# A planned fp32 attention and MoE kernel: new costs in the plan, idle transposes as filler, and one addition moved from ACT to DVE

## The chip, the cores and the metric

The kernel runs on one core of a Trainium2 chip. The metric is device microseconds of an execution; lower is better. The engines are PE (TensorE, matmuls and transposes), DVE (VectorE), ACT (ScalarE), POOL (GpSimd) and SP (SyncE, which here issues the DMAs). Each engine works through its own queue in order and waits at an instruction for the semaphores of others.

## What is computed

```
scores = q @ k.T / sqrt(64), causal mask, softmax:  attn = exp(s - max) / (sum + 1e-9)
x = (attn @ v) of 2 x 12 heads, 448 positions, 64 wide   -> 896 tokens x 768
x = ((x @ w1) * (x @ w2)) @ w3 @ w_out                   (768 -> 1024 -> 1024 -> 768)
h = x @ v_in ;  out = (h * clip(h + 3, 0, 6) / 6) @ v_out  (768 -> 2048 -> 768)
```

All weights arrive as 64-bit floats and are turned on the chip into pairs of fp32 parts, high and low. A dense product is three matmuls on these parts.

## The kernel before, in words

Attention works on 12 units of two heads each. A unit has seven score tiles `s_6` to `s_0` (128 rows, 448 down to 64 columns). For each, PE makes the scores in one of three PSUM banks (L431), DVE takes the scaled and masked minimum (L434), and ACT takes the exponential and its sum (L438). For tiles 6 to 4 and then 3 to 0, ACT adds 1e-9 to the sums (L450), DVE takes the reciprocal (L452), and POOL scales the exponentials in place (L458, tile `prb`). PE then transposes 16 blocks in four groups `ptp_0` to `ptp_3` (L480), ACT and DVE copy them out (L488, L492), and PE multiplies by v (`o`, L505).

Beside it runs the product `w3 @ w_out` (`pw`, 384 matmuls, L568), whose weights are loaded (L255) and converted by ACT, DVE and POOL (L261 to L295: L292 shifts the low word, L295 joins the words, L261 and L267 split the result). What of `pw` doesn't fit beside attention follows it. Then come the dense parts: `pa` (x @ w1 and x @ w2, by Strassen's scheme, L703), `px` (L812), `pg` (L703) and `po` (L877).

The order of instructions on each engine is not written out by hand. A planner, `Plan`, records every operation with an engine, an assumed cost in us, what it reads and writes, and a rank. `issue` then plays it through: whichever engine is free first takes, of its operations whose inputs are ready, the one of lowest rank, and the instructions are emitted in that order. So a changed cost moves instructions on every engine. `LATENCY` is what a result takes to reach another engine. PSUM and SBUF buffers go round in rings; an operation that opens a buffer waits for the last reader of the one before in it. Before any of this, `setup` makes the identity and issues 20 transposes of it (L410, tile `warm`).

Of the kernel before, what the change touches and what calls it, by code (L numbers as in the profile page):

```python
# [9 lines left out]
F32 = mybir.dt.float32  # L10
# [12 lines left out]
DENSE_BANKS = 2  # L23
# [25 lines left out]

WARM = 20  # L50
SHAPE = (2, 12, 448, 64)
# [21 lines left out]
class Plan:  # L73
# [3 lines left out]

    LATENCY = {"pe": 0.2, "sp": 2.2}

    def __init__(self):  # L80
        self.ops = []
        self.tags = {}

    def tile(self, make, tag, bufs, after=()):
        return Handle(self, make, tag, bufs, after)

    def op(self, eng, cost, fn, reads=(), writes=(), rank=0.0, after=()):
        i = len(self.ops)
        deps = set(after)
        args = [(*(a if isinstance(a, tuple) else (a, None)), w)  # L90
# [15 lines left out]
    def issue(self):  # L106
        n = len(self.ops)
        deps = [set(o[3]) for o in self.ops]
        for bufs, hs in self.tags.values():
            for x, h in enumerate(hs):  # L110
                first = h.uses[0][0]
                if x >= 1:
                    deps[first].add(hs[x - 1].uses[0][0])
# [15 lines left out]
        here = {e: [] for e in engines}  # L129
        free = {e: 0.0 for e in engines}  # L130
        for i in range(n):
            if not left[i]:
                heapq.heappush(coming[self.ops[i][0]], (0.0, i))
        for _ in range(n):
            t, e = min(
                (free[e] if here[e] else max(free[e], coming[e][0][0]), e)
                for e in engines if here[e] or coming[e]
            )
# [5 lines left out]
            free[e] = t + self.ops[i][1]  # L144
            for j in after[i]:
                near = self.ops[j][0] == e and e != "sp"
                ready[j] = max(ready[j], free[e] + (0.0 if near else self.LATENCY.get(e, 0.12)))
                left[j] -= 1
                if not left[j]:
                    heapq.heappush(coming[self.ops[j][0]], (ready[j], j))  # L150
        return max(free.values())
# [3 lines left out]
def attention_moe_moe2(ctx: ExitStack, tc, q, k, v, w1, w2, w3, w_out, v_in, v_out, out):  # L155
# [102 lines left out]
    def split(plan, hl, at_, size, x, reads, rank, eng="dve"):  # L258
# [5 lines left out]
        else:  # L264
# [3 lines left out]
            hl[:, LO, at_:at_ + size], x(), f32(hl[:, HI, at_:at_ + size]), ALU.subtract),  # L268
            reads=[*reads, hl.at(("h", at_))], writes=[hl.at(("l", at_))], rank=rank)

# [6 lines left out]
    def bits(plan, raw, size, rank, shifted=False, packed=False):  # L277
# [12 lines left out]
        else:  # L290
            plan.op("dve", 0.16 + size * 0.00052,
                    lambda: nc.vector.tensor_single_scalar(lo(), lo(), 29, ALU.logical_shift_right),  # L292
                    writes=[lb], rank=rank)
        to = (lambda: flat(raw)[:, :size]) if packed else lo
        plan.op("dve", dve(size), lambda: nc.vector.scalar_tensor_tensor(  # L295
            to(), hi(), 3, lo(), ALU.logical_shift_left, ALU.bitwise_or),
            reads=[] if packed else [hb], writes=[lb, hb] if packed else [lb], rank=rank)

# [24 lines left out]
    def combine(plan, f, r1, r2, rank):  # L323
# [20 lines left out]
        def add(dst, reads, write, a, b, op):  # L344
            plan.op("dve", dve(h), lambda: nc.vector.tensor_tensor(dst(), a(), b(), op),
                    reads=reads, writes=[write], rank=rank)

# [38 lines left out]
    def load(u):  # L386
# [4 lines left out]
        vr[u] = tile_of("vr", 3, [P, 4, 2, D], f"vr{u}")  # L391
        plan.op("sp", 0.6, lambda: nc.sync.dma_start(qs[u][:, :], q[u]), writes=[qs[u]], rank=rank)
        plan.op("sp", 0.6, lambda: nc.sync.dma_start(ks[u][:, :], k[u]), writes=[ks[u]], rank=rank)
        plan.op("sp", 0.6, lambda: nc.sync.dma_start(vr[u][:, :], v[u]), writes=[vr[u]], rank=rank)

# [47 lines left out]
    def normalise(u, t0, t1):  # L443
# [51 lines left out]
    def p_v(u):  # L495
# [32 lines left out]
        xt[p, b] = t  # L528

    setup()  # L530
    for u in range(n_u):
# [424 lines left out]
```

## Time and profile before

| | |
|---|---|
| median of 3 runs | 553.81 us (553.14 to 557.26) |
| the profiled execution | 556.21 us, its span 554.4 us |
| PE busy | 540.8 us (98%), 2828 matmuls |
| DVE, ACT, POOL busy | 388.9, 301.6, 108.0 us |
| HBM | 75.24 MB read, 14.16 MB written |

Busy times are of the profiled execution. PE's matmuls overlap in the pipeline, so its busy time alone does not say that it works at its peak; the pace between starts, and the clock that it was granted, say more. The time in front of an instruction on which its engine did nothing is put down to whatever released it last.

### The profile page before, as it was taken

To read this page: it belongs to the slowest core of one execution; us is meant where nothing else is said; L and a number is where in the kernel's file an instruction comes from. 1 tells how busy PE (TensorE), PEld (TensorE's weight loads), DVE (VectorE), ACT (ScalarE), POOL (GpSimd) and SP (SyncE) were. 2 spreads that over 40 slices of the span, in tenths; PEclk is the share of its full clock that TensorE was granted. 3 is DMA by queue.
4 is the path that set the end of the run, shared out by engine and by line. 5 is a ranking of instruction groups with operands and counts; after the bars stand their busy time and mean duration, and the time that the engine had idled before them with its cause. 6 is when DMAs were issued, how large, how long until landed. Compare 5 with 4: busy or idle time off the path is not lost.

```text
span 554.4 us, 7965 instructions
## 1 busy us (share of the span) xinstructions
PE 540.8 (98%) x2828; PEld 480.3 (87%) x2828; DVE 388.9 (70%) x722; ACT 301.6 (54%) x606; POOL 108.0 (19%) x150
## 2 busy tenths in 40 slices
PE   7899999999999999999999999999999999999997
PEld 5576657778999999999999999999999999899996
DVE  3677777764962789888747549999978884876322
ACT  4587886785822555564526335996846651653000
POOL 4656456553101111111000102010101000000000
PEclk9899999999999999999999999999999999999999
DMA  8666785722713143422433011357384846572664
GB/s 314 245 201 228 226 278 206 232 92 72 228 44 96 61 151 145 156 99 97 170 96 115 0 58 67 124 209 240 110 314 139 276 164 194 175 252 80 204 188 143
DMA packets 33224, 89.91 MB, mean 162 GB/s; under 512 B 3232, under 2 KB 21664, under 8 KB 30624
## 3 DMA queue, kind: packets, MB, share of 16 engines
q1 hardware_dynamic: 33184, 89.40, 47.7%
q8 instruction: 22, 0.36, 0.3%
q14 instruction: 18, 0.15, 0.1%
HBM read 75.24 MB, written 14.16 MB: 161 GB/s over the span
## 4 chain that ended last, share of the span: by engine, by line
PE 75%; DVE 1%; issue 0%; ACT 0%; DVEq 0%
PE po L877 21%; PE paX L703 10%; PE px L812 10%; PE pgX L703 10%; PE pw L568 7%; PE paZ L703 5%; PE pgZ L703 5%; PE pgY L703 3%; PE paY L703 3%; PE o L505 0%; PE ptp L480 0%; DVE o L671 0%; DVE vja L267 0%; DVE q L841 0%; ACT q L838 0%
## 5 line engine op out<-in xcount | busy, mean ns | idle before, releaser
L877 PE MATMUL po<-g,vo 128*128 128x448 f32 x576 | 116.3, 362 | 0.0
L877 PEld LDWEIGHTS po<-g,vo 128*128 128x128 f32 x576 | 108.0, 187 | 7.2
L568 PE MATMUL pw<-wr,w 128*128 128x384 f32 x384 | 75.8, 347 | 0.0
L458 POOL TENSOR_SCALAR prb<-prb,sums 128x448 f32<-128x448 f32 (+6 forms) x84 | 59.5, 725 | 54.9 <-DVE sums L452 54.9
L568 PEld LDWEIGHTS pw<-wr,w 128*128 128x128 f32 x384 | 65.9, 188 | 1.7
L812 PE MATMUL px<-ab,wp 128*128 128x448 f32 x288 | 57.9, 362 | 0.0
L812 PEld LDWEIGHTS px<-ab,wp 128*128 128x128 f32 x288 | 54.0, 187 | 3.6
L431 PE MATMUL s<-ks,qs 128*128 128x448 f32 (+6 forms) x168 | 51.2, 415 | 4.3 <-DMA ks<-in_k 2.2
L671 DVE TENSOR_TENSOR o<-po,o 128x448 f32<-128x448 f32 x36 | 22.4, 623 | 40.7 <-PE po L877 38.9
L438 ACT ACTIVATE prb<-z,sums 128x448 f32<-128x448 f32 (+6 forms) x84 | 42.1, 506 | 5.6 <-DVE sums L434 5.5
L434 DVE CUSTOM_DVE_ANT_0 z<-s,maskb 128x448 f32<-128x448 f32 (+6 forms) x84 | 33.3, 418 | 15.7 <-PE s L431 11.4
L431 PEld LDWEIGHTS s<-ks,qs 128*128 128x128 f32 x168 | 28.4, 197 | 14.8 <-DVE sums L434 5.7
L261 POOL TENSOR_SCALAR vja<-vir 128x768 fp32r<-128x768 f32 x8 | 7.3, 914 | 169.6 <-DVE x2t L653 70.2
L488 ACT COPY pt<-ptp 128x512 f32<-128x512 f32 (+1 forms) x48 | 24.7, 562 | 15.8 <-PE ptp L480 15.6
L480 PEld LDWEIGHTS ptp<-ident,prb 128*128 128x128 f32 x192 | 22.4, 143 | 9.7 <-POOL prb L458 5.3
L480 PE MATMUL ptp<-ident,prb 128*128 128x128 f32 x192 | 26.4, 280 | 4.2 <-POOL prb L458 4.2
L505 PE MATMUL o<-pt,vr 128*64 128x448 f32 (+3 forms) x192 | 26.9, 396 | 0.0
L505 PEld LDWEIGHTS o<-pt,vr 128*64 128x64 f32 (+1 forms) x192 | 10.9, 134 | 17.5 <-issue 11.9
L265 ACT CAST vo<-vor 128x1024 fp32r<-128x1024 f32 x12 | 13.6, 1136 | 17.3 <-PE po L877 15.3
L285 ACT ACTIVATE vor<-vor 128x1024 f32<-128x1024 f32 x12 | 13.9, 1158 | 15.9 <-DMA vor<-in_moe_w_out 15.9
L664 DVE SCALAR_TENSOR_TENSOR g<-rab,g 128x448 fp32r<-128x448 f32 x32 | 20.6, 650 | 1.6 <-ACT g L662 1.6
L662 ACT ACTIVATE g<-rab 128x448 fp32r<-128x448 f32 x32 | 18.2, 576 | 5.4 <-DVE rab L660 5.4
(146 smaller groups left out, 1038.2 us busy)
## 6 DMA issues: line engine op xcount, KB each, us to landing
vor<-in_moe_w_out SPq DMA_DIRECT2D x12, 1024.0 KB, 5.6
w3r<-in_moe_w SPq DMA_DIRECT2D x8, 1024.0 KB, 6.6
sums_of<-o SPq DMA_DIRECT2D x36, 224.0 KB, 3.1
o<-sums_of SPq DMA_DIRECT2D x36, 224.0 KB, 2.8
wrr<-in_moe_w_out SPq DMA_DIRECT2D x8, 768.0 KB, 5.5
w1r<-in_moe_w SPq DMA_DIRECT2D x8, 768.0 KB, 5.6
w2r<-in_moe_w SPq DMA_DIRECT2D x8, 768.0 KB, 4.2
vjr<-in_moe_w_in SPq DMA_DIRECT2D x8, 768.0 KB, 5.0
```

What stands on the lines that cost most here:

```text
L431: plan.op("pe", pe4(n), lambda: nc.tensor.matmul(ps[:, :n], qs[u][:, t].rearrange("p h i -> p (h i)"), ks[u][:, :n], start=True, stop=True ...
L434: plan.op("dve", dve(n) + 0.09, lambda: nc.vector.tensor_tensor_reduce(out=z[:, :n], in0=ps[:, :n], in1=maskb[:, S - n:], scale=-SCALE, sc ...
L438: plan.op("act", act(n, True) + 0.2, lambda: nc.scalar.activation(pb[:, OFF[t]:OFF[t] + n], z[:, :n], AF.Exp, bias=sm[:, 0, t:t + 1], scal ...
L458: nc.gpsimd.tensor_scalar(s, s, sm[:, 1, t:t + 1], 1.0, ALU.mult, ALU.mult)
L480: nc.tensor.transpose(ps[:w, i * P:(i + 1) * P], pb[:, OFF[t] + kb * P:OFF[t] + kb * P + w], ident)
L488: plan.op("act", act(cut), lambda: nc.scalar.copy(dst()[:, :cut], ps[:, :cut]), reads=[ps], writes=[d.at((g, 0))], rank=rank)
L505: nc.tensor.matmul(ps[T * j:T * j + T, kb * P:S], vr[u][:w, kb, j, :], d[:w, base[kb]:base[kb] + TQ - 2 * kb, j, :], start=kb == 0, stop=k ...
L568: nc.tensor.matmul(ps[:, :W], weight(n, a, kk), hls[1 + kk][:, c, h * W:(h + 1) * W], start=kk == 0 and a == c, stop=kk == KF - 1 and a == LO)
L671: plan.op("dve", dve(S), lambda: nc.vector.tensor_tensor(o[:, :], ps[:, :S], o[:, :], ALU.add), reads=[ps], writes=[o], rank=rank)
L703: nc.tensor.matmul(ps[:, :S], hl[:, a, off + kk * P:off + (kk + 1) * P], t[:, c], start=first and kk == 0 and a == c, stop=kk == HK - 1 an ...
L812: nc.tensor.matmul(ps[m, b][:, :S], weight(n, a, kk), ab[kk][:, c, cols(b)], start=kk == 0 and a == c, stop=kk == KF - 1 and a == LO)
L877: nc.tensor.matmul(ps[:, :S], hls[n][:, a, at_:at_ + P], gt[k][:, d, cols(b)], start=kk == 0 and a == d, stop=kk == KC - 1 and a == LO)
```

## The change

Five things are changed.

1. The planner's costs. An engine can now start late (`START`: PE at 5.0 us, SP at 0.6). The loads of q, k and v cost 1.3, 0.7 and 0.8 us of SP instead of 0.6 each.
2. POOL's stands. DVE operations marked `ports=True` (those with two SBUF inputs, and the shift L292) lock POOL: one that POOL has begun ends later by their cost, and one that begins starts when they have ended. Two SP operations that are tied only by the order of a ring no longer have `LATENCY` between them.
3. The addition of 1e-9 goes from ACT (rank `early`) to DVE, ahead of the reciprocal.
4. `keep_warm` puts 60 transposes of the identity on PE with rank 1000, the last of all, into a bank of the ring that `pw` uses, and allows them from the first score on.
5. The transposes ahead of the first score become 18.

The core of the diff (the marks `ports=True` stand on L267, L292, L295, L345 and the differences of L597, too):

```diff
-WARM = 20
+WARM = 18
+
+FILL, IDLE = 60, 1000.0
...
     LATENCY = {"pe": 0.2, "sp": 2.2}
+    START = {"pe": 5.0, "sp": 0.6}
...
-        free = {e: 0.0 for e in engines}
+        free = {e: self.START.get(e, 0.0) for e in engines}
...
+        busy, locked = None, 0.0
+
+        def settle(i, end):
+            e = self.ops[i][0]
+            for j in after[i]:
+                near = self.ops[j][0] == e and (e != "sp" or (i, j) in order)
+                ready[j] = max(ready[j], end + (0.0 if near else self.LATENCY.get(e, 0.12)))
...
+            if busy and busy[1] <= t:
+                settle(*busy)
+                busy = None
+                continue
...
+            cost = self.ops[i][1]
+            if e == "pool":
+                free[e] = max(t, locked) + cost
+                busy = i, free[e]
+                continue
+            free[e] = t + cost
+            if i in self.ports:
+                locked = free[e]
+                if busy:
+                    free["pool"] = busy[1] + cost
+                    busy = busy[0], free["pool"]
+            settle(i, free[e])
...
-        plan.op("sp", 0.6, lambda: nc.sync.dma_start(qs[u][:, :], q[u]), writes=[qs[u]], rank=rank)
-        plan.op("sp", 0.6, lambda: nc.sync.dma_start(ks[u][:, :], k[u]), writes=[ks[u]], rank=rank)
-        plan.op("sp", 0.6, lambda: nc.sync.dma_start(vr[u][:, :], v[u]), writes=[vr[u]], rank=rank)
+        plan.op("sp", 1.3, lambda: nc.sync.dma_start(qs[u][:, :], q[u]), writes=[qs[u]], rank=rank)
+        plan.op("sp", 0.7, lambda: nc.sync.dma_start(ks[u][:, :], k[u]), writes=[ks[u]], rank=rank)
+        plan.op("sp", 0.8, lambda: nc.sync.dma_start(vr[u][:, :], v[u]), writes=[vr[u]], rank=rank)
...
-        early = u + (TQ - 1 - t0) * 0.05 + RANK["exp"]
         total = [sm.at((2, t)) for t in range(t0, t1)]
-        plan.op("act", 0.22, lambda: nc.scalar.activation(
-            sm[:, 2, t0:t1], sm[:, 1, t0:t1], AF.Copy, bias=1.0e-9, scale=1.0), reads=acc, writes=total, rank=early)
+        plan.op("dve", 0.17, lambda: nc.vector.tensor_single_scalar(sm[:, 2, t0:t1], sm[:, 1, t0:t1], 1.0e-9, ALU.add),
+                reads=acc, writes=total, rank=rank)
...
+    def keep_warm(after):
+        ps = plan.tile(lambda: pd.tile([P, 512], F32, tag="d", name="warm"), "psd", DENSE_BANKS)
+        for i in range(FILL):
+            plan.op("pe", 0.11, lambda: nc.tensor.transpose(ps[:, :P], ident, ident), writes=[ps], rank=IDLE, after=after)
...
     attended = len(plan.ops)
+    keep_warm([min(i for i in range(attended) if plan.ops[i][0] == "pe")])
```

What this does to the order is shown at three places. The first is the start of the kernel, on SP and DVE. `qs1`, `ks1` and `vr1` are q, k and v of unit 1, `w3r0` and `wrr0` the first raw weights. SP before:

```order
L392 DMA qs0_132<-in_q 128x896
L393 DMA ks0_134<-in_k 128x448
L394 DMA vr0_136<-in_v 128x512
L255 DMA w3r0_138<-in_moe_w3 128x2048
L392 DMA qs1_147<-in_q 128x896
L393 DMA ks1_156<-in_k 128x448
L394 DMA vr1_162<-in_v 128x512
```

SP after:

```order
L424 DMA qs0_130<-in_q 128x896
L425 DMA ks0_132<-in_k 128x448
L426 DMA vr0_134<-in_v 128x512
L424 DMA qs1_136<-in_q 128x896
L425 DMA ks1_138<-in_k 128x448
L426 DMA vr1_142<-in_v 128x512
L287 DMA w3r0_149<-in_moe_w3 128x2048
```

The three loads of unit 1 have moved ahead of `w3r0`. On DVE, `z0_2` is the minimum of score tile 2 of unit 0, and the row `sums0` behind it reads it out. DVE before, from the first `w3r0` operation on:

```order
L292 TENSOR_SCALAR w3r0_138<-w3r0_138 128x1024
L434 ISA z0_2_176,sums0_145<-s0_2_160,maskb_86 128x192
L434 ISA sums0_145 128x1
L434 ISA z0_1_179,sums0_145<-s0_1_167,maskb_86 128x128
L434 ISA sums0_145 128x1
L452 RECIPROCAL sums0_145<-sums0_145 128x3
L295 SCALAR_TENSOR_TENSOR w3r0_138<-w3r0_138 128x1024
```

DVE after, from the minimum of tile 4 of unit 1 on:

```order
L466 ISA z1_4_219,sums1_202<-s1_4_199,maskb_86 128x320
L466 ISA sums1_202 128x1
L481 TENSOR_SCALAR sums0_147<-sums0_147 128x4
L483 RECIPROCAL sums0_147<-sums0_147 128x4
L324 TENSOR_SCALAR w3r0_149<-w3r0_149 128x1024
L327 SCALAR_TENSOR_TENSOR w3r0_149<-w3r0_149 128x1024
L466 ISA z1_3_260,sums1_202<-s1_3_215,maskb_86 128x256
```

The two `w3r0` operations stand behind the second reciprocal of unit 0 now, and the new addition (L481) stands ahead of it.

The second place is PE from the middle of unit 1's scores to the first transposes of unit 0. Before:

```order
L431 MATMUL s1_3_213<-ks1_156,qs1_147 128x256
L431 MATMUL s1_2_219<-ks1_156,qs1_147 128x192
L431 MATMUL s1_1_223<-ks1_156,qs1_147 128x128
L431 MATMUL s1_0_236<-ks1_156,qs1_147 128x64
L480 MATMUL ptp0_0_238<-ident_85,prb0_87 128x128 x4
L480 MATMUL ptp0_1_247<-ident_85,prb0_87 128x128 x4
L431 MATMUL s2_6_257<-ks2_193,qs2_189 128x448
```

After:

```order
L463 MATMUL s1_3_215<-ks1_138,qs1_136 128x256
L564 MATMUL warm_160<-ident_85 128x128 x2
L463 MATMUL s1_2_222<-ks1_138,qs1_136 128x192
L564 MATMUL warm_160<-ident_85 128x128 x2
L463 MATMUL s1_1_229<-ks1_138,qs1_136 128x128
L564 MATMUL warm_160<-ident_85 128x128 x24
L463 MATMUL s1_0_271<-ks1_138,qs1_136 128x64
L564 MATMUL warm_160<-ident_85 128x128 x7
L463 MATMUL s2_6_288<-ks2_227,qs2_211 128x448
L511 MATMUL ptp0_0_298<-ident_85,prb0_87 128x128 x4
L511 MATMUL ptp0_1_307<-ident_85,prb0_87 128x128 x4
```

35 of the 60 idle transposes stand in these rows, 14 ahead of them and 11 behind, and the first score of unit 2 has moved ahead of the transposes.

The third place is PE in the middle of attention, at the first transposes of unit 3 (`ptp3`). Before:

```order
L431 MATMUL s4_3_546<-ks4_375,qs4_369 128x256
L568 MATMUL pw0_1_331<-wr3_513,w30_201 128x384 x3
L431 MATMUL s4_2_555<-ks4_375,qs4_369 128x192
L431 MATMUL s4_1_559<-ks4_375,qs4_369 128x128
L480 MATMUL ptp3_0_571<-ident_85,prb1_88 128x128 x4
L480 MATMUL ptp3_1_579<-ident_85,prb1_88 128x128 x4
L431 MATMUL s4_0_587<-ks4_375,qs4_369 128x64
L431 MATMUL s5_6_590<-ks5_468,qs5_457 128x448
```

After:

```order
L463 MATMUL s4_2_592<-ks4_417,qs4_397 128x192
L605 MATMUL pw0_0_449<-wr2_518,w30_294 128x384 x3
L463 MATMUL s4_1_603<-ks4_417,qs4_397 128x128
L605 MATMUL pw0_1_500<-wr2_518,w30_294 128x384 x3
L463 MATMUL s4_0_615<-ks4_417,qs4_397 128x64
L605 MATMUL pw0_0_449<-wr3_590,w30_294 128x384 x3
L463 MATMUL s5_6_631<-ks5_545,qs5_525 128x448
L511 MATMUL ptp3_0_643<-ident_85,prb1_88 128x128 x4
L511 MATMUL ptp3_1_651<-ident_85,prb1_88 128x128 x4
```

The transposes of unit 3 now stand behind `s4_0`, three more `pw` matmuls and `s5_6`. Of the `pw` matmuls 165 stood ahead of the last `o` before, and 156 do now.

## Rows read from the trace of the kernel before

**Rows 1.** The page: busy time of each engine.
```profile
PE 540.8 (98%) x2828; PEld 480.3 (87%) x2828; DVE 388.9 (70%) x722; ACT 301.6 (54%) x606; POOL 108.0 (19%) x150
```

**Rows 2.** Stretches: busy us and count of each engine; granted clock; DMA share and GB/s.
```profile
core 0: us, PE busy (x) PEld busy (x) DVE busy (x) ACT busy (x) POOL busy (x), PEclk, DMA share, GB/s
11.10:12.00 0.90, 0.89 (x2) 0.47 (x3) 0.71 (x3) 0.78 (x5) 0.90 (x1) 0.85 1.02 423
12.00:15.00 3.00, 3.00 (x7) 1.77 (x6) 1.35 (x5) 1.98 (x7) 2.27 (x4) 0.50 1.03 398
...
16.00:19.00 3.00, 0.43 (x2) 0.30 (x2) 3.00 (x13) 1.04 (x5) 3.00 (x5) 0.93 0.39 100
19.00:22.00 3.00, 2.92 (x10) 2.44 (x11) 0.45 (x1) 1.50 (x4) 2.83 (x5) 0.51 1.00 388
...
22.00:140.00 118.00, 114.39 (x699) 83.01 (x698) 82.99 (x236) 88.95 (x254) 63.07 (x87) 1.00 0.58 191
140.00:554.40 414.40, 410.64 (x2074) 385.40 (x2073) 295.50 (x450) 201.12 (x324) 31.96 (x33) 1.00 0.43 146
...
470.00:475.00 5.00, 4.84 (x23) 3.88 (x23) 4.67 (x6) 2.02 (x5) 1.36 (x1) 1.00 0.48 154
```

**Rows 3.** Timeline of PE, first 23 us: start, us, what, count, [idle before it <-releaser].
```profile
1.36 4.11 PE L410 MATMUL warm<-ident 128*128 128x128 f32 x20 [1.36 <-POOL ident masks.py:199]
5.31 3.60 PE L431 MATMUL s<-ks,qs 128*128 128x448 f32 x14
11.12 4.84 PE L431 MATMUL s<-ks,qs 128*128 128x448 f32 x12 [2.21 <-DMA ks<-in_k]
16.94 0.43 PE L431 MATMUL s<-ks,qs 128*128 128x64 f32 x2 [0.98 <-DVE sums L434]
19.08 1.97 PE L480 MATMUL ptp<-ident,prb 128*128 128x128 f32 x8 [1.70 <-POOL prb L458]
20.84 2.13 PE L431 MATMUL s<-ks,qs 128*128 128x448 f32 x4
```

**Rows 4.** Timeline of SP and DVE at the start; the two `ks` loads' time to landing.
```profile
1.17 0.42 SPq L393 DMA_DIRECT2D ks<-in_k  x1
3.06 0.45 SPq L393 DMA_DIRECT2D ks<-in_k  x1
...
DMA to landing us min/median/max: 3.4/5.6/7.9
...
9.25 0.70 DVE L292 TENSOR_SCALAR w3r<-w3r 128x1024 uint32<-128x1024 uint32 x1 [0.83 <-DMA w3r<-in_moe_w]
15.26 0.17 DVE L452 RECIPROCAL sums<-sums 128x4 f32<-128x4 f32 x1
```

**Rows 5.** Timeline of PE in the middle of attention.
```profile
37.50 1.04 PE L480 MATMUL ptp<-ident,prb 128*128 128x128 f32 x8
38.38 0.97 PE L431 MATMUL s<-ks,qs 128*128 128x448 f32 x2
...
47.80 1.09 PE L480 MATMUL ptp<-ident,prb 128*128 128x128 f32 x8 [1.11 <-POOL prb L458]
```

**Rows 6.** Waits of PE, whole span: us in total, times, longest us.
```profile
PE ptp L480 <- POOL prb L458: 4.2, 4, 1.7
PE s L431 <- DVE sums L434: 1.9, 3, 1.0
```

**Rows 7.** POOL's groups by form, 10 to 14 us (busy us, mean ns), and DVE's timeline.
```profile
L458 POOL TENSOR_SCALAR prb<-prb,sums 128x448 f32<-128x448 f32 x1 | 1.6, 1560 | 6.8 <-DVE sums L452 6.8
L458 POOL TENSOR_SCALAR prb<-prb,sums 128x384 f32<-128x384 f32 x1 | 0.6, 582 | 0.0
...
10.45 1.22 DVE L295 SCALAR_TENSOR_TENSOR w3r<-w3r 128x1024 uint32<-128x1024 uint32 x1
15.35 1.19 DVE L267 TENSOR_TENSOR w<-w3r,w 128x1024 fp32r<-128x1024 f32 x1
```

**Rows 8.** Lines L450 and L452: ns min/median/max; who waited for L452 (us, times).
```profile
L450 ACT ACTIVATE sums<-sums x24: 207/208/226, 9.0 to 126.8; 128x3 f32<-128x3 f32 x12, 128x4 f32<-128x4 f32 x12
L452 DVE RECIPROCAL sums<-sums x24: 156/170/179, 10.3 to 127.0; 128x3 f32<-128x3 f32 x12, 128x4 f32<-128x4 f32 x12
...
  POOL prb L458: 54.9, 21
```

**Rows 9.** Chain of waits in order of time: start us, us, what.
```profile
136.82 38.17 PE pw L568 x219
174.99 1.80 PE paX L703 x9
...
550.82 0.02 issue
```

More of the change, by code (lines that the diff above doesn't have):

```diff
@@ L82, in __init__, with op @@
         self.tags = {}
+        self.ports = set()
     def tile(self, make, tag, bufs, after=()):
         return Handle(self, make, tag, bufs, after)
-    def op(self, eng, cost, fn, reads=(), writes=(), rank=0.0, after=()):
+    def op(self, eng, cost, fn, reads=(), writes=(), rank=0.0, after=(), ports=False):
         i = len(self.ops)
+        if ports:
+            self.ports.add(i)
         deps = set(after)
@@ L108, in issue @@
         deps = [set(o[3]) for o in self.ops]
+        order = set()
         for bufs, hs in self.tags.values():
@@ L112, in issue @@
                 if x >= 1:
-                    deps[first].add(hs[x - 1].uses[0][0])
+                    before = hs[x - 1].uses[0][0]
+                    if before not in deps[first]:
+                        order.add((before, first))
+                    deps[first].add(before)
                 if x >= bufs:
@@ L133, in issue @@
                 heapq.heappush(coming[self.ops[i][0]], (0.0, i))
-        for _ in range(n):
-            t, e = min(
+        busy, locked = None, 0.0
[4 more added lines that the diff above has]
+                ready[j] = max(ready[j], end + (0.0 if near else self.LATENCY.get(e, 0.12)))
+                left[j] -= 1
+                if not left[j]:
+                    heapq.heappush(coming[self.ops[j][0]], (ready[j], j))
+        todo = n
+        while todo or busy:
+            t, e = min((
                 (free[e] if here[e] else max(free[e], coming[e][0][0]), e)
                 for e in engines if here[e] or coming[e]
-            )
+            ), default=(float("inf"), None))
+            if busy and busy[1] <= t:
+                settle(*busy)
+                busy = None
+                continue
             while coming[e] and coming[e][0][0] <= t:
@@ L143, in issue @@
             self.ops[i][2]()
[L144 to L150, printed above, removed]
+            todo -= 1
+            cost = self.ops[i][1]
[10 more added lines that the diff above has]
+            settle(i, free[e])
         return max(free.values())
@@ L268, in split @@
             hl[:, LO, at_:at_ + size], x(), f32(hl[:, HI, at_:at_ + size]), ALU.subtract),
-            reads=[*reads, hl.at(("h", at_))], writes=[hl.at(("l", at_))], rank=rank)
+            reads=[*reads, hl.at(("h", at_))], writes=[hl.at(("l", at_))], rank=rank, ports=True)
     def parts(name, m):
@@ L292, in bits @@
                     lambda: nc.vector.tensor_single_scalar(lo(), lo(), 29, ALU.logical_shift_right),
-                    writes=[lb], rank=rank)
+                    writes=[lb], rank=rank, ports=True)
         to = (lambda: flat(raw)[:, :size]) if packed else lo
@@ L296, in bits @@
             to(), hi(), 3, lo(), ALU.logical_shift_left, ALU.bitwise_or),
-            reads=[] if packed else [hb], writes=[lb, hb] if packed else [lb], rank=rank)
+            reads=[] if packed else [hb], writes=[lb, hb] if packed else [lb], rank=rank, ports=True)
     def convert(plan, n, rank):
@@ L345, in add @@
             plan.op("dve", dve(h), lambda: nc.vector.tensor_tensor(dst(), a(), b(), op),
-                    reads=reads, writes=[write], rank=rank)
+                    reads=reads, writes=[write], rank=rank, ports=True)
         L1, L2, H1, H2 = r1.at("l"), r2.at("l"), r1.at("h"), r2.at("h")
@@ L597, in difference @@
         plan.op("dve", dve(S), lambda: nc.vector.tensor_tensor(dst(), a(), b(), op),
-                reads=reads, writes=[write], rank=FORM)
+                reads=reads, writes=[write], rank=FORM, ports=True)
     def moving(name, p, x, reads):
@@ L604, in moving @@
         plan.op("dve", dve(S), lambda: nc.vector.tensor_tensor(t[:, LO], x(), f32(t[:, HI]), ALU.subtract),
-                reads=[*reads, t.at(0)], writes=[t.at(1)], rank=FORM)
+                reads=[*reads, t.at(0)], writes=[t.at(1)], rank=FORM, ports=True)
         tt[name, p] = t
```

## The prediction

> **What bounds the kernel now.** I read the page first, then TensorE's part of the timeline, its granted clock in a table of stretches, the list of waits, and last the chain of waits. PE is busy for 540.8 of 554.4 us, so only its losses can be won [rows 1]. They lie unevenly. From 140 us to the end PE is busy 410.64 of 414.40 us, and 3.6 us of the difference are the last evictions and stores behind its last matmul at 550.8; the chain is one row of matmuls, 219 of `pw` in 38.17 us and then 9 in 1.80 us again and again [rows 2, 9]. Nothing is to be had there. Between 22 and 140 us, attention with `pw` matmuls as filler, it is busy 114.39 of 118.00 us: 3.6 us of gaps [rows 2]. The first 22 us are the poor stretch.
>
> In these, PE does 20 warm-up transposes, then the seven scores of unit 0, which end at 5.31 + 3.60 = 8.91. It then stands until 11.12, because the keys of unit 1 are not there (2.21 us, released by the DMA of `ks`); again 0.98 us before the last score of unit 1; and again 1.70 us until POOL has scaled the block that the first transposes read [rows 3]. Together 4.9 us of standing. After the first of these stands the granted clock falls to 0.50 (1.2 GHz instead of 2.4) and is there from 12 to 15 us; after the others it is at 0.51 from 19 to 22. PE's busy time in each stretch times what the clock lacks: 0.89 x 0.15 + 3.00 x 0.50 + 0.43 x 0.07 + 2.92 x 0.49 = 3.1 us [rows 2]. So the start loses 4.9 + 3.1 = 8.0 us. Transposes show what the level means: eight take 38.38 - 37.50 = 0.88 us at full clock (0.11 each), and 20.84 - 19.08 = 1.76 at half (0.22) [rows 3, 5].
>
> **The change, part by part.** *Order of the loads.* In the queue of SP, q, k and v of unit 1 now stand ahead of the 1024 KB of `w3r0`. Before, `ks0` was issued at 1.17 and landed 3.4 us later, at 4.57; `ks1` was issued at 3.06 and landed 7.9 us later, at 10.96 [rows 4]. Between the two landings lay 256 + 1024 + 448 + 224 = 1952 KB (from the shapes in the order), in 6.39 us. Without `w3r0` it is 928 KB, so an estimated 3.0 us: `ks1` lands at about 7.6, before unit 0's scores and their fills end (about 9.4). The 2.21 us wait goes. `w3r0` itself, which was there at 9.25, has 928 KB more ahead of it and comes an estimated 2 to 3 us later. Its DVE work has moved behind the second reciprocal; before, it stood in DVE's queue and waited 0.83 us for the transfer, with the minima of two score tiles behind it [rows 4].
>
> *POOL's stands.* A scaling of 448 columns took 1560 ns where a DVE op with two SBUF inputs (L295, 1.22 us from 10.45) ran beside it, and the 384 columns after it 582 ns alone: POOL stood for about 1.0 us [rows 7]. The plan now adds this to POOL's time, so it expects normalised blocks later and puts other work ahead of the transposes. By the order, with the durations of such instructions in the timeline, PE's work between `s_0` of a unit and `ptp_0` of the same unit grows from 8.5 us to 10.9 on the mean of the 12 units. At unit 3, the third place of the order, `s4_0`, `s5_6` and a group of three `pw` have come ahead of them: the 448 columns alone are 0.8 us (the row at 38.38). That is what should close the gaps of the middle: of the 3.6 us, 2.5 are transposes waiting for POOL (4.2 in all, less the 1.70 of the start) and 0.9 are scores waiting for DVE to free a bank (1.9 less 0.98) [rows 3, 6]. An example is the 1.11 us at 47.80 [rows 5]. Bounds: all gaps go (0), or new ones as long as the old come (3.6). I take 1.5 left: the POOL part nearly gone, the bank part as before. Gain 2.1.
>
> *The idle transposes.* Sixty more instructions on PE, 60 x 0.11 = 6.6 us at full clock [rows 5]. All are in the order by the fourth unit's first score, 31 of them just ahead of the first `s2_6` and `ptp0`. They don't wait for other engines but hold everything behind them, since PE's queue is in order. At nothing they would cost only where PE stands anyway. I count them in full, since PE has more work than the others by then. It comes to the first `ptp0` at about 5.0 + 2 x 3.6 (two units' scores) + 49 x 0.11 + 0.8 (`s2_6`) = 18.4 us. POOL took 19.08 - 15.43 = 3.65 us from the end of the second reciprocal to the first transposes; that reciprocal now comes after `s1_4`, about 12.5 us, and with the 0.70 and 1.22 us of the two `w3r0` ops beside POOL in place of one of 1.19 it is done about 17 us [rows 3, 4, 7]. What they buy is the clock: no stand, no fall, so the 3.1 us go with the 4.9. Bounds of what PE still stands: 0, and the old 0.98 + 1.70; I take 0.3, near the first, because PE is the late one at both places.
>
> *Two warm-up transposes less.* 20 take 4.11 us, 0.2 each [rows 3]; the keys of unit 0 land at 4.57 and the scores began at 5.31, so up to 0.4 us is won. I take 0.4 (bounds 0 and 0.4).
>
> *1e-9 on DVE.* 24 ACT instructions of 208 ns go (5.0 us of ACT), 24 small ones come on DVE; their like is the reciprocal, 170 ns, so 4.1 us of DVE [rows 8]. Between 22 and 140 us DVE is busy 82.99 and ACT 88.95 of 118 us [rows 2], so both hide it; the way from the last exponential to the reciprocal keeps its one change of engine. Zero, and under the rival below what it costs if it isn't hidden.
>
> *The dense part.* PE's order after attention is the old one but for two groups of `pg` matmuls; DVE, ACT and SP are reshuffled. Attention takes 156 `pw` matmuls along instead of 165; the nine others cost 9 x 0.174 = 1.6 us later (38.17 / 219) and as much less before, so nothing in the sum [rows 9]. DVE's conversions still have 228 x 0.174 = 39.7 us of `pw` as cover where they had 38.2. Zero, with 0.7 either way: PE's known stand there is 0.16 us, 4.84 busy of 5.00 from 470 to 475 us, and it is as easily doubled as lost [rows 2].
>
> **The sum.** Start: -8.0 + 6.6 + 0.3 - 0.4 = -1.5. Middle: -2.1. Together -3.6 us. The profiled execution took 556.2 us (span 554.4), 2.4 above the median of the three runs shown, 553.8; a change of this size carries over, so 553.8 - 3.6 = **550.2 us**.
>
> **A rule against it.** The rows say that transposes alone do raise the clock: the warm-up ran at 0.2 us a transpose, near the half-clock pace, and the seven scores right behind it took 3.60 us, where unit 1's first six needed 4.84 with the clock at 0.50 [rows 2, 3]. The Trainium skill, page "TensorE: Matmul & The Clock Gate", section "Part 4: PE-mode transpose", says the contrary: work in transpose mode doesn't count as TensorE being busy, and full clock isn't reached by it. By the rule the fills would buy nothing; by the rows they hold the clock. I go by the rows, and keep the other case as a rival.
>
> **Rivals.**
> 1. *The clock falls all the same* in the first 25 us, for as long as before, because PE is as idle as before between its scores. Then the 3.1 us stay: 550.2 + 3.1 = 553.3, no difference to be measured. For it: fills come in twos to fours in unit 0 and 1, and a stand can lie between them. Against it: the 31 in one piece stand just where the second fall began, and the scores after the warm-up were fast. Chance 0.11. The Trainium skill's rule above, from the same page and section, would have this outcome.
> 2. *The fills delay less than they take, and all gaps close.* 1.5 more from the middle, 0.3 from the start, and some 1.0 where the chunks of `pw`, `o` and transposes need fewer changes of kind: 547.4. For it: PE's distance to POOL grows in 11 of 12 units. Against it: PE's work is then all that is left, and nothing in the rows makes that shorter. Chance 0.20.
> 3. *The chain exponential, sum, reciprocal, POOL becomes the bound* (the other side). The sum now needs DVE twice, in order, behind conversions of 1.2 us (L295), and POOL already waits 54.9 us for L452, 21 times [rows 7, 8]. If each of the 11 later units got one wait like the 1.11 us at 47.80, the middle would have 12.2 us of gaps where it has 3.6: 553.8 - 1.5 + 8.6 = 560.9. It beats the gain of the start from (3.6 + 1.5) / 11 = 0.46 us a unit on. Against it: the 2.4 us of distance that the order adds. Chance 0.08 for 1% and more, 0.07 for a smaller loss.
> 4. *The change moves the order but not the sum*: gaps of 3.6 us again in other places, because the plan's durations are still not the chip's. 553.8 - 1.5 = 552.3. Chance 0.12.
>
> **How the numbers follow.** My forecast, 549 to 552, holds 0.42, rivals 1 and 4 0.23, rival 2 0.20, rival 3 0.15. Within 1% (548.3 to 559.3; about what a measurement here can tell from no change) lie the forecast, rivals 1 and 4, the smaller loss of 3, and a fifth of 2: 0.42 + 0.23 + 0.07 + 0.04 = 0.76. Faster 0.16, slower 0.08. The range goes from rival 2 less the 0.7 of the dense part, 546.7, to rival 1 with that 0.7 and the 0.3 that I took for the start, 554.3; outside lie most of rival 3 and the far tail of rival 2, some 0.2.
>
> **What would show it right or wrong.** Start: the score of unit 1 follows unit 0's within 0.5 us with no wait for the DMA; granted clock 1.00 from 6 to 140 us; the 60 fills at 0.11 us each; the first `ptp` at about 18 instead of 19.08, with 49 fills ahead of it. Middle: PE's gaps from 26 us to the end of attention sum to 1 to 2 us, most behind DVE. Dense part: px still in 57 us, the same pace. Wrong if the clock shows 0.50 again, if `w3r0` or `wrr0` is what DVE waits for with scores behind it, if POOL is waited for at most `ptp_0`, or if PE stands at the first `pw` because its weights are converted later than before.

## The result, and the profile after

| | before | after |
|---|---|---|
| median, first comparison | 554.32 us (553.14 to 557.26, 4 runs) | 548.67 us (547.97 to 548.95, 4 runs) |
| the profiled execution, its span | 556.21, 554.4 us | 548.48, 546.5 us |
| PE busy | 540.8 us, 2828 matmuls | 540.0 us, 2886 matmuls |
| DVE, ACT, POOL busy | 388.9, 301.6, 108.0 us | 397.0, 298.2, 113.5 us |

The ratio is 0.9875, interval 0.9844 to 0.9906: 5.65 us or 1.2% faster. Two later comparisons of the same two kernels, on other chips, gave 0.9838 (0.9806 to 0.9870) and 0.9916 (0.9887 to 0.9945). So the change wins about one per cent (0.8 to 1.6), at the very bound between "within 1%" and "faster". The time lies inside the predicted range, 1.5 us below the predicted 550.2 and 1.3 above rival 2's 547.4.

The first lines to look at are PE's timeline at the start, after (start, us, what, count, idle time before it); they answer [rows 3].

```profile
1.36 4.10 PE L442 MATMUL warm<-ident 128*128 128x128 f32 x18 [1.36 <-POOL ident masks.py:199]
5.25 3.03 PE L463 MATMUL s<-ks,qs 128*128 128x448 f32 x8
...
9.94 2.10 PE L463 MATMUL s<-ks,qs 128*128 128x448 f32 x6
...
13.73 2.78 PE L564 MATMUL warm<-ident 128*128 128x128 f32 x24
16.35 0.33 PE L463 MATMUL s<-ks,qs 128*128 128x64 f32 x2
16.52 0.94 PE L564 MATMUL warm<-ident 128*128 128x128 f32 x7
17.30 0.92 PE L463 MATMUL s<-ks,qs 128*128 128x448 f32 x2
18.05 1.04 PE L511 MATMUL ptp<-ident,prb 128*128 128x128 f32 x8
```

No row has an idle time behind it after the first 1.36 us. Unit 1's first score is at 9.94 instead of 11.12, with no wait for its keys, and the first transposes are at 18.05 instead of 19.08 with 49 fills ahead of them. Twenty-four fills take 16.35 - 13.73 = 2.62 us, 0.109 each.

The stretches of after, with the columns of [rows 2]: busy us and count of PE, PEld, DVE, ACT and POOL, granted clock, DMA share, GB/s.

```profile
12.00:15.00 3.00, 3.00 (x27) 2.88 (x26) 2.85 (x9) 2.93 (x5) 1.85 (x2) 1.00 1.03 398
16.00:19.00 3.00, 3.00 (x25) 2.58 (x24) 2.97 (x10) 1.48 (x7) 2.60 (x4) 1.00 0.51 147
19.00:22.00 3.00, 3.00 (x20) 2.45 (x20) 2.26 (x8) 3.00 (x8) 1.17 (x3) 1.00 0.33 127
22.00:140.00 118.00, 116.44 (x733) 89.33 (x731) 95.49 (x266) 88.97 (x236) 71.86 (x89) 1.00 0.63 210
140.00:546.50 406.50, 402.91 (x2034) 378.67 (x2032) 288.30 (x436) 195.87 (x311) 30.25 (x32) 1.00 0.43 145
```

The clock is 1.00 in the three stretches where it was 0.50, 0.93 and 0.51. From 22 to 140 us PE's gaps have shrunk from 3.61 to 1.56 us. All of it is one gap. PE's waits (us, times, longest) and the rows of PE and DVE at that place:

```profile
PE s L463 <- DVE sums L466: 1.6, 1, 1.6
```

```profile
62.41 1.02 PE L463 MATMUL s<-ks,qs 128*128 128x448 f32 x2 [1.55 <-DVE sums L466]
```

```profile
61.39 0.70 DVE L324 TENSOR_SCALAR w3r<-w3r 128x1024 uint32<-128x1024 uint32 x1 [1.83 <-DMA w3r<-in_moe_w]
```

POOL is not waited for at all any more (4.2 us in [rows 6]). What is left is like the case that the prediction named as a danger for `w3r0`, only with a later one of these weights: DVE stands 1.83 us for a `w3r` transfer, with score minima queued behind that operation, and the next score finds no free bank. The length of this gap differs from one execution of the same kernel to the next: it is 1.15 us in the profile of e8 and 0.95 in that of e10, both the changed kernel again.

The new addition is cheap (median 166 ns), and POOL waits less for what follows it. The row of L481 has ns min/median/max; the row below it says how long, and how often, POOL waited for the reciprocal L483 (before: 54.9, 21 times [rows 8]).

```profile
L481 DVE TENSOR_SCALAR sums<-sums x24: 151/166/1085, 9.6 to 117.6; 128x3 f32<-128x3 f32 x12, 128x4 f32<-128x4 f32 x12
```

```profile
  POOL prb L489: 23.5, 13
```

The chain of waits has the same shape as in [rows 9]: `pw` behind attention, now 228 of them and 8.5 us earlier, at the same pace (39.72 / 228 = 0.174).

```profile
128.31 39.72 PE pw L605 x228
```

One number can only be understood with the granted clock of each execution. The 37 executions of before that the three later comparisons measured differ in their mean granted clock, and the lower it is the longer they take:

| mean granted clock of the execution | executions of before | median (lowest to highest) |
|---|---|---|
| 0.999 to 1.000 | 4 | 552.5 us (551.3 to 553.2) |
| 0.996 to 0.997 | 14 | 554.4 us (552.9 to 556.3) |
| 0.993 to 0.994 | 12 | 556.7 us (555.3 to 558.8) |
| 0.989 to 0.991 | 7 | 557.1 us (556.0 to 557.8) |

Of the 12 executions of the changed kernel 11 were at 0.998 to 1.000 (547.3 to 549.9 us), and one at 0.996 (550.6). What a mean of 0.994 lacks, over 554 us, is 3.3 us, close to the 3.1 us that the prediction worked out, and the mean of all 37 lacks 2.9. But the profiled execution of before was one of the 0.994 group, and its 556.21 us lay 1.9 us above the median of the first comparison. So the two spans differ by 7.9 us and the medians by 5.65. In the later comparisons the medians differ by 8.2 us (before mostly at 0.993 to 0.994) and 5.6 (mostly at 0.996 to 1.000).

### The profile page after: what moved, and what is told of

Its sections match the earlier page's. It is cut to its first block, busy times and chain, and to the rows that moved or that the text cites. A ratio compares the mean times of both kernels' runs of the same rounds, so it can differ in the third digit from the quotient of the medians.

```text
span 546.5 us, 8100 instructions
## 1 busy us (share of the span) xinstructions
PE 540.0 (99%) x2886; PEld 485.6 (89%) x2886; DVE 397.0 (73%) x746; ACT 298.2 (55%) x582; POOL 113.5 (21%) x150
## 4 chain that ended last, share of the span: by engine, by line
PE 95%; DVE 2%; DMA 1%; issue 0%; ACT 0%; POOL 0%; POOLq 0%; DVEq 0%
PE po L914 21%; PE pw L605 12%; PE pgX L740 11%; PE px L849 11%; PE paX L740 11%; PE s L463 6%; PE pgZ L740 5%; PE paZ L740 5%; PE o L536 4%; PE ptp L511 3%; PE pgY L740 3%; PE paY L740 3%; DMA w3r<-in_moe_w 1%; PE warm L564 1%; PE warm L442 1%; DVE z L466 1%
## 5 line engine op out<-in xcount | busy, mean ns | idle before, releaser
L914 PEld LDWEIGHTS po<-g,vo 128*128 128x128 f32 x576 | 108.0, 187 | 7.2
L489 POOL TENSOR_SCALAR prb<-prb,sums 128x448 f32<-128x448 f32 (+6 forms) x84 | 65.2, 792 | 38.9 <-DVE sums L483 23.5
L463 PE MATMUL s<-ks,qs 128*128 128x448 f32 (+6 forms) x168 | 48.7, 394 | 1.6 <-DVE sums L466 1.6
L611 ACT COPY g<-pw 128x384 f32<-128x384 f32 x16 | 7.7, 481 | 24.2 <-PE pw L605 14.6
```

Source lines behind the costliest of these rows:

```text
L463: plan.op("pe", pe4(n), lambda: nc.tensor.matmul(ps[:, :n], qs[u][:, t].rearrange("p h i -> p (h i)"), ks[u][:, :n], start=True, stop=True ...
L489: nc.gpsimd.tensor_scalar(s, s, sm[:, 1, t:t + 1], 1.0, ALU.mult, ALU.mult)
L914: nc.tensor.matmul(ps[:, :S], hls[n][:, a, at_:at_ + P], gt[k][:, d, cols(b)], start=kk == 0 and a == d, stop=kk == KC - 1 and a == LO)
```

## The experiments

Each kernel is named by its label. "After" is the changed kernel; the diffs are against it, but for one.

### Do the fills hold the clock, and at what price? e1, e2, e7

In e1 the order of all instructions is that of after, but the 60 fills issue nothing.

```diff
-            plan.op("pe", 0.11, lambda: nc.tensor.transpose(ps[:, :P], ident, ident), writes=[ps], rank=IDLE, after=after)
+            plan.op("pe", 0.11, lambda: None, writes=[ps], rank=IDLE, after=after)
```

> The changed kernel with its order untouched, but the 60 idle transposes issue nothing (a planned place, no instruction); the result is still the reference's. The changed kernel took 548.7 us. Theory (the fills hold the clock, and of their 6.6 us about 2.9 stand in the way: 1.7 ahead of the first ptp0, which came at 18.05 where POOL was done at 16.3, and 1.2 ahead of unit 2's p.v): without them PE stands again between unit 1's scores, the granted clock shows 0.50 for a stretch between 12 and 22 us, and what is won in front of ptp0 is lost at half clock: 547.5 to 549.5. Rival (the clock would hold anyway, since the early keys of unit 1 took the stands away): no 0.50 anywhere, first ptp0 at about 16.4, 545.8.

It took 546.76 us (546.23 to 547.72), ratio 0.9860 (0.9818 to 0.9902): below the theory's range by number, but with the fall of the clock that the theory named and the rival excluded. PE's timeline, its first `o`, and a stretch:

```profile
14.89 0.43 PE L463 MATMUL s<-ks,qs 128*128 128x64 f32 x2 [2.14 <-DVE sums L466]
15.63 1.02 PE L463 MATMUL s<-ks,qs 128*128 128x448 f32 x2 [0.31 <-DVE sums L466]
16.49 1.82 PE L511 MATMUL ptp<-ident,prb 128*128 128x128 f32 x8
18.11 2.29 PE L463 MATMUL s<-ks,qs 128*128 128x384 f32 x4
```

```profile
21.95 2.10 PE L536 MATMUL o<-pt,vr 128*64 128x448 f32 x16
```

```profile
16.50:20.00 3.50, 3.50 (x13) 2.70 (x12) 1.96 (x4) 2.33 (x6) 2.73 (x4) 0.51 0.56 198
```

PE stands 2.14 us where the long piece of fills was, and then the clock is at 0.51: eight transposes take 18.11 - 16.49 = 1.62 us at half speed, against 0.87 in after. So the fills do hold the clock. All four executions of e1 had 0.995 to 0.997. Yet e1 is by its median 1.9 us below after's first, though measured on another chip; by way of e2, with which each was compared on one chip (below), it is 2.45 - 1.5, about 1 us. So the 60 fills cost more than the clock they save.

In e2 only the fills numbered 18 to 48 are issued, the 31 around the last score of unit 1. e7 issues the first 24 of them (`18 <= i < 42`).

```diff
+            fn = lambda: nc.tensor.transpose(ps[:, :P], ident, ident)
+            plan.op("pe", 0.11, fn if 18 <= i < 49 else lambda: None, writes=[ps], rank=IDLE, after=after)
```

> The changed kernel with its order untouched, but of the 60 idle transposes only the 31 in the one long piece ahead of the first s2_6 are issued; the 18 ahead of them and the 11 behind are left out. Theory (fills count in full wherever PE has other work): the 11 behind cost 11 x 0.11 = 1.2 us, the 18 ahead up to 2.0; clock stays at 1.00, and the time is 545.5 to 547.5. Rival (the small pieces hold the clock too, between scores that wait for banks): 0.50 shows before 16 us and the time is 548.5 or more.

> The changed kernel with its order, but only the 24 idle transposes ahead of s1_0 are issued. e2 with 31 took 545.3 us. Theory (the 7 behind s1_0 stand in the way by up to 0.8 us, as PE comes to ptp0 at 17.14 and POOL is done at about 16): 544.5 to 545.0, no fall of the clock. Rival (PE then waits for the bank of s2_6 or for POOL as long): 545.3, the same.

e2 took 545.26 us (545.06 to 545.35), ratio 0.9831 (0.9791 to 0.9870), beside e1 on one chip. Its waits, two rows of PE and a stretch:

```profile
PE s L463 <- DVE sums L466: 0.3, 1, 0.3
```

```profile
17.14 1.04 PE L511 MATMUL ptp<-ident,prb 128*128 128x128 f32 x8
20.93 2.10 PE L536 MATMUL o<-pt,vr 128*64 128x448 f32 x16
```

```profile
15.00:20.00 5.00, 5.00 (x37) 4.11 (x36) 4.88 (x17) 4.33 (x16) 4.53 (x7) 1.00 0.76 277
```

The clock stays at 1.00 with the 31 alone, and the gap near 62 us is gone in this profile too (in that of e9, the same kernel, it is 0.70). Against e1 the 31 fills put off the first transposes by 0.65 us (17.14 and 16.49), but at full clock the first `o` comes at 20.93 instead of 21.95; the medians differ by 1.5 us. So 31 are worth their price, and the 29 others aren't. They don't cost 0.11 us each everywhere: the 23 of them ahead of the first `o` take 2.5 us, but put it off from 20.93 (e2 and e9) to 21.80, 22.38 and 22.77 (e10, after, e8), 0.9 to 1.8 us. e7 took 546.47 us (545.45 to 548.16), ratio 0.9818 (0.9785 to 0.9850), with a clock of 1.00, two small stands at the start (below) and one of 0.5 us at 59 us:

```profile
9.11 3.36 PE L463 MATMUL s<-ks,qs 128*128 128x448 f32 x12 [0.46 <-DVE sums L481]
16.06 1.02 PE L463 MATMUL s<-ks,qs 128*128 128x448 f32 x2 [0.55 <-DVE sums L466]
```

Its span, 543.5 us, is that of e2, 543.4, so the half microsecond that the theory expected isn't there. One of its four executions had a mean clock of 0.995 and was the slowest (548.16); all eight of e2 and e9 had 0.999 to 1.000. Otherwise nothing could be told apart between 24 and 31.

e2 was run again beside after itself, on one chip.

> The kernel with only the 31 idle transposes that stand in one piece ahead of the first s2_6, once more, on one chip with the changed kernel itself. Theory (the 29 others, in pieces of one to four, are paid for one by one at 0.11 us, and 18 of them also push the place of the w3r0 operations so that PE stands 1.5 us once): 2.5 to 3.5 us less than the changed kernel in the same comparison. Rival (the difference of the two earlier comparisons was one of the chips and of the clock's rise at the start, 4.9 or 6.2 us): under 1 us less.

> The changed kernel as it is, beside the one with 31 fills. 548 to 549 us; one gap of 1.1 to 1.6 us at the scores near 62 us, behind DVE.

546.19 us (545.24 to 548.23) against 548.64 (547.81 to 550.56): 2.45 us less, just under what the theory expected and above the rival's 1 us; 29 x 0.11 is 3.2. The executions overlap a little, four on each side. e2 has the lowest times found, 0.9831 and 0.9876 of before; e7 (0.9818) can't be told from it.

### What is the planning of POOL's stands worth? e3

```diff
-            self.ports.add(i)
+            pass
```

> The changed kernel with POOL's stands taken out of the plan (no operation is marked); all else as changed. Theory (the gain in the middle of attention, some 4 us by the trace, comes from planning these stands): PE waits for POOL at several ptp again, 2 to 4 us in all, and the time is 551 to 553. Rival (it comes from the addition on DVE and the other costs): gaps stay at 1.6 us and the time within 0.7 of 548.7.

552.60 us (550.43 to 553.31, 10 runs), ratio 0.9937 (0.9911 to 0.9963): about 3.9 us of the gain are lost (against after's first median, on another chip). PE's waits, and its three gaps:

```profile
PE ptp L511 <- POOL prb L489: 3.4, 3, 2.1
```

```profile
15.81 1.09 PE L511 MATMUL ptp<-ident,prb 128*128 128x128 f32 x8 [0.72 <-POOL prb L489]
73.41 1.09 PE L511 MATMUL ptp<-ident,prb 128*128 128x128 f32 x8 [2.13 <-POOL prb L489]
103.52 1.09 PE L511 MATMUL ptp<-ident,prb 128*128 128x128 f32 x8 [0.55 <-POOL prb L489]
```

The transposes wait for POOL again, 3.4 us as against one gap of 1.55 behind DVE in after. That is 1.9 us. The rest shows in the ten executions: the three with a clock of 0.998 to 1.000 took 550.4 to 550.9 us, the seven with 0.995 to 0.997 took 552.4 to 553.3. The profiled one is of the first kind, so its trace has no fall. That it is the stand of 2.13 us that makes the clock fall in the others is inferred: no profile of such an execution was taken here.

### Where does the 1e-9 matter? e4

The addition goes back to ACT, with its old rank; all else stays.

```diff
-        plan.op("dve", 0.17, lambda: nc.vector.tensor_single_scalar(sm[:, 2, t0:t1], sm[:, 1, t0:t1], 1.0e-9, ALU.add),
-                reads=acc, writes=total, rank=rank)
+        plan.op("act", 0.22, lambda: nc.scalar.activation(
+            sm[:, 2, t0:t1], sm[:, 1, t0:t1], AF.Copy, bias=1.0e-9, scale=1.0), reads=acc, writes=total, rank=u + (TQ - 1 - t0) * 0.05 + RANK["exp"])
```

> The changed kernel with the addition of 1e-9 back on ACT at its old rank; all else as changed. Theory (ACT and DVE both hide it, it is worth nothing): 548.2 to 549.2. Rival (5 us less on ACT and one instruction less between its exponentials is part of the gain in the middle): 550 to 551, with PE waiting more for ACT or POOL.

549.65 us (548.23 to 550.86), ratio 0.9898 (0.9863 to 0.9934), 1.0 us above after's first median and overlapping with its executions. Its profile has 2.3 us of waits for a bank, where after has 1.6:

```profile
PE s L463 <- DVE sums L466: 2.3, 4, 1.1
```

So the move is worth about a microsecond or nothing. It lies between the two expectations, and isn't settled more closely than that.

### Who brings the keys of unit 1 early? e5, e6

In the plan after, two SP operations that are tied only by a ring's order need no `LATENCY` between them. e5 takes that out of after; e6 puts it, and nothing else, into before.

```diff
-                near = self.ops[j][0] == e and (e != "sp" or (i, j) in order)
+                near = self.ops[j][0] == e and e != "sp"
```

> The changed kernel without one rule of its plan: two SP operations tied only by the order of a ring get the 2.2 us between them again. By the order this alone puts w3r0 back ahead of q, k and v of unit 1 (the new costs of the loads do not move it), and the fills fall otherwise: 17 ahead of s1_6. Theory (early keys of unit 1 were worth about 2 us of standing, now partly filled by transposes): ks1 lands at about 11 again, PE stands or fills until then, the first ptp0 comes at 18.5 to 20, the clock holds by the fills, 549.5 to 551. Rival (the start is bound by ACT and POOL anyway): within 0.7 of 548.7.

> The kernel before with that rule alone added: q, k and v of unit 1 are loaded ahead of w3r0; no fills, no marks for POOL, the addition on ACT. Theory (the first stand, 2.21 us, and the first fall of the clock, 1.6 us, go; the stand in front of the first transposes and its fall stay): 1.5 to 3 us faster than before. Rival (what PE wins it waits for at POOL): less than 0.7 us.

e5: 550.61 us (548.66 to 551.01), ratio 0.9882 (0.9851 to 0.9914), 2.6 us above after on the same chip (e8, below). Unit 1's first score comes at 11.33 instead of 9.94, and the fills stand in the hole in its place, so the clock holds:

```profile
9.46 2.03 PE L564 MATMUL warm<-ident 128*128 128x128 f32 x17
11.33 1.56 PE L463 MATMUL s<-ks,qs 128*128 128x448 f32 x4
```

The prediction gave the earlier loads to the new order as a whole; this shows that the ring rule makes it, not the new load costs.

e6: 556.37 us (554.99 to 559.55, 10 runs), ratio 1.0009 (0.9982 to 1.0037). The rule alone wins nothing, where the theory expected 1.5 to 3 us. PE's timeline, and a row of DVE, tell why:

```profile
13.11 0.70 PE L435 MATMUL s<-ks,qs 128*128 128x256 f32 x2 [2.16 <-DVE sums L438]
14.78 1.40 PE L435 MATMUL s<-ks,qs 128*128 128x192 f32 x4 [0.97 <-DVE sums L438]
17.04 0.69 PE L435 MATMUL s<-ks,qs 128*128 128x64 f32 x2 [0.86 <-DVE sums L438]
18.30 1.97 PE L484 MATMUL ptp<-ident,prb 128*128 128x128 f32 x8 [0.57 <-POOL prb L462]
```

```profile
11.82 0.70 DVE L296 TENSOR_SCALAR w3r<-w3r 128x1024 uint32<-128x1024 uint32 x1 [2.02 <-DMA w3r<-in_moe_w]
```

```profile
15.00:21.00 6.00, 4.57 (x16) 3.67 (x17) 4.35 (x16) 3.64 (x12) 6.00 (x8) 0.50 0.79 274
```

The DMA wait of 2.21 us is gone, and PE stands 2.16 + 0.97 + 0.86 us for DVE a few scores later. DVE itself stands 2.02 us for the transfer of `w3r0`, which comes later now, with the minima of unit 1 behind it. The clock falls as before. So the earlier keys pay nothing while DVE's `w3r0` work stands where it stood. Fills aren't needed for them to pay: e1 has none, and its first transposes are at 16.49 instead of 19.08.

After itself was run beside these.

> The changed kernel itself, beside the others on this chip, for their comparison: 548 to 549.5 us, PE's one gap in the middle again where DVE waits for the transfer of a w3r.

548.02 us (547.28 to 549.90), ratio 0.9838 (0.9806 to 0.9870).

### The transposes ahead of the first score: e11, e12

`WARM` is 20 in e11 and 0 in e12, instead of 18.

> The changed kernel with 20 transposes ahead of the first score instead of 18. The prediction's step: the first score is waited for by these transposes, so two more of them cost 0.4 us, and the scores begin at 5.66 instead of 5.25. Rival (the first score waits for the keys, which land at about 4.6 to 5, or the scores behind it run at half pace until the clock rises, so an earlier begin is worth only half of it): 0 to 0.2 us.

> The changed kernel with no transposes ahead of the first score, nothing else changed. If the transposes at the start are what raises the clock (what the rows of both kernels suggest), the scores of unit 0 begin at about 4.6 to 5.0 and run at half pace for some 4 us longer: 3 to 4 us later at the first score of unit 1 less the 0.3 to 0.6 of the earlier begin, so 1 to 2 us slower than the changed kernel. If transposes count for nothing there (the Trainium skill, page "TensorE: Matmul & The Clock Gate", section "Part 4: PE-mode transpose") the clock rises when it rises in the changed kernel, and it is 0 to 0.5 us faster.

e11, beside e10 on one chip: 548.07 us (547.47 to 548.95), ratio 0.9902 (0.9878 to 0.9926), so two more transposes cost nothing that can be measured; but 0.4 us couldn't be told here, as the executions of each differ by more. e12: 549.53 us (548.07 to 551.82), ratio 0.9923 (0.9895 to 0.9950), 0.9 us slower than e10 by the medians, with executions that overlap. The first eight score matmuls of e11, and then of e12:

```profile
5.68 2.98 PE L463 MATMUL s<-ks,qs 128*128 128x448 f32 x8
```

```profile
5.00 4.31 PE L463 MATMUL s<-ks,qs 128*128 128x448 f32 x8 [5.00 <-DMA ks<-in_k]
```

In e12 they begin 0.25 us earlier than in after (the keys land at 5.00), but take 4.31 us instead of 3.03, and unit 1's first score comes at 10.97 instead of 9.94. Nothing but identity transposes was taken away, so it is these that bring the faster clock earlier; three profiles of the changed kernel have 2.53 to 3.42 us for these eight (last section). In e12's profile there is no gap at 62 us, which makes up for part of it in its span, 546.1 us.

## Why the prediction was right where it was, and where it failed

| step | forecast, us | measured, us |
|---|---|---|
| stands at the start | -4.9 + 0.3 | -4.9, none left |
| clock at the start | -3.1 | -3.1 in the profiled pair, -2.9 against the mean of before's 37 executions, about -1.9 (0.0035 x 554) against the largest group |
| 60 fills | +6.6 | +6.5 of PE's time (60 x 0.109); 29 left out give back 2.45, not 3.2 |
| two warm-ups fewer | -0.4 | -0.06 at the begin of the scores, no effect told in the times |
| gaps, 22 to 140 us | -2.1 | 3.61 - 1.56: -2.05 (1.15 and 0.95 us left in e8, e10) |
| PE's own work, attention | 0 | -1.3 located, some 2 more not |
| dense part | 0, with 0.7 either way | -0.9 in the profiled pair, +0.6 and 0.0 with e8 and e10 |
| sum | -3.6 | spans -7.9, medians -5.65 |

The dense part is the time from the first `pa` matmul to the end of the span: 554.4 - 174.99 = 379.4 us in before [rows 9], 546.5 - 168.03 = 378.5 in after, 380.0 in e8 and 379.5 in e10. So its zero held. The row of after:

```profile
168.03 1.80 PE paX L740 x9
```

**Right: the start.** No wait for the keys, the clock at 1.00, fills at 0.11 us, the first transposes at 18.05 where 18 was forecast. The step that counted the fills in full was the one that rival 2 doubted. As a count of PE's time it holds, since no stand is left and each fill takes 0.109 us; as what the fills add to the time it is too much, for 23 of them put the first `o` off by 0.9 to 1.8 us and not 2.5. That the fills take away the stands is right only in part: in e1, without any, 2.14 + 0.31 us of stands are left of the old 4.9, and the first transposes come 1.56 us earlier than in after. The rest of the stands went with the new order. e2 and e9 show that nearly half of the fills bought nothing.

**Right: going by the rows against the rule.** The rows of e1 and e12 show it: without the fills the clock is at 0.51 after a stand of PE, with them at 1.00; without the transposes at the start the scores run at half pace for longer. The Trainium skill, page "TensorE: Matmul & The Clock Gate", section "Part 4: PE-mode transpose", says that work in transpose mode doesn't count as TensorE being busy in the same way, from a measurement with bf16; no run here agrees with that for these fp32 transposes. The profile prints them as MATMUL, and doesn't show whether they run in that mode. Rival 1 is thereby out.

**Right in size: the middle's gaps.** 1.56 us are left where 1.5 was taken, and the POOL part is gone. e3 shows that it is the planning of POOL's stands that does it. POOL's collisions with DVE are not fewer for it (it is busy 113.5 us instead of 108.0); PE has other work meanwhile. The other half is luck: the prediction left the old waits for a bank in place, and these are gone; the 1.56 is a new one behind a transfer, which with the same order was 0.95 to 1.7 us long in e8, e10 and e11 and absent in e12. The 1.0 us that POOL stood in the prediction's example is 0.9, since 448 columns alone take 639 ns in after; the sum doesn't use it. Rival 3, the sum's chain over DVE, didn't come: POOL waits 23.5 us for the reciprocal instead of 54.9, and e4 without the move is no faster. Rival 4 is out with the gaps.

**Failed: "Two warm-up transposes less", 0.4 us.** The scores begin at 5.25 instead of 5.31. The warm-up ran at half pace until its end (4.10 us for 18; in before 4.11 for 20), because the clock rose later in this execution, and the first scores paid. The bound was too high, too: in e12, without any, the scores wait for the keys until 5.00, so 0.3 is the most that could be won. Whether two transposes cost anything stays open: unit 1's first score is at 10.32 in e11, with 20, and at 9.36, 9.94 and 10.33 in e10, after and e8, with 18.

**Mis-sized: the clock.** The prediction took 3.1 us from a profiled execution and subtracted it from a median of others. The table of executions shows that this loss differs from one execution to the next. As a mean of before's executions it is about right (2.9); but the 553.8 from which it was taken lies at the level of the largest group, 554.4, which lacks 1.9. For this comparison it should have been about -1.9, with the rest in the range; the clocks of its other executions of before are not on record, so this is read from their times.

**Mis-sized: PE's own work, which the prediction held to be constant.** By the page, before's 540.8 us busy less 3.1 of half clock, plus 58 more transposes of 0.11, would be 544.1; after has 540.0. The same work takes 4.1 us less. Part of it is the neighbours in PE's order. Two scores of 320 columns between their neighbours, in before and in after:

```profile
69.96 1.51 PE L505 MATMUL o<-pt,vr 128*64 128x448 f32 x8
71.40 0.81 PE L431 MATMUL s<-ks,qs 128*128 128x320 f32 x2
72.14 0.81 PE L505 MATMUL o<-pt,vr 128*64 128x192 f32 x8
```

```profile
27.89 0.60 PE L511 MATMUL ptp<-ident,prb 128*128 128x128 f32 x4
28.32 0.70 PE L463 MATMUL s<-ks,qs 128*128 128x320 f32 x2
28.86 0.60 PE L511 MATMUL ptp<-ident,prb 128*128 128x128 f32 x4
```

72.14 - 71.40 = 0.74 us between `o` and `o`, and 28.86 - 28.32 = 0.54 between transposes: 0.1 us for each side on which a score meets `o`. Counted over the trace, scores and `o` are neighbours 31 times in before, 18 in after, 19 in e2 and 29 in e3. 13 fewer are 1.3 us, which rival 2 had put at 1.0. About 2 us of the 4.1 are neither this nor the dense part; they are spread over attention, and no run here isolates them. No edit moved the neighbours alone, so their price is read from rows and not tested; e3 bears it out by half at best: with 11 more such neighbours than e10, the same 2886 matmuls and first scores as fast, its PE is busy 0.5 us more (540.2 and 539.7), not 1.1.

**The chances.** 0.76 on "within 1%" and 0.16 on faster was too sure: the forecast lay 0.65% below before, and one unseen term of 3 us, PE's own work, was enough to bring the time to the bound. That the forecast came within 1.5 us is in part luck, as the clock, taken 1.2 us too high, and PE's own work, left at nothing, err in opposite directions. The range's lower end, 546.7, came from rival 2 and held.

## What to carry to other kernels

Idle transposes paid here in one place only, the hole in which PE otherwise stood 2.14 us and its clock fell to 0.51: look for that one hole (31 fills, worth 1.5 us), and leave the rest empty. A plan gains when it knows what makes an engine stand (here DVE's two-input operations for POOL), more than when it knows transfer times alone: in this kernel the earlier load by itself only moved the wait to DVE. Before a clock loss of a profiled execution goes into a sum, look how that execution's mean clock stands among the others.

## What the runs showed of the hardware that was not expected

The time at which the clock first rises is not fixed: the first eight score matmuls, started at 5.25 and 5.26 us, took 3.03 us in after and 3.42 in e8, the same kernel, where they are 2.53 in e10 (from 5.17):

```profile
5.26 3.42 PE L463 MATMUL s<-ks,qs 128*128 128x448 f32 x8
```

```profile
5.17 2.53 PE L463 MATMUL s<-ks,qs 128*128 128x448 f32 x8
```

The granted clock is printed as 1.00 in these first microseconds in all of them; only the pace of the matmuls shows the half speed.

The clock can fall late, too, with the other engines in full work. In e6 it was at 100 us, behind one stand of PE:

```profile
100.29 0.69 PE L435 MATMUL s<-ks,qs 128*128 128x64 f32 x2 [2.12 <-DVE sums L438]
```

```profile
100.20:103.50 3.30, 3.21 (x13) 3.08 (x14) 2.73 (x9) 0.56 (x1) 0.00 (x0) 0.50 0.41 118
```

In e3 a stand of the same length, 2.13 us, left it at 1.00 in the profiled execution. What decides between the two is open.
